# Keys scaled on GpSimd, transfers begun by SP, planned durations reset and weight conversions reordered in a three-layer kernel

## The chip, the cores and the metric

The kernel runs on one core of one Trainium2 chip. The metric is device time in microseconds of the whole program, the median over runs. "Before" and "after" are the kernel without and with the change. Engines are named TensorE (PE in the profile, PEld for its weight loads), VectorE (DVE), ScalarE (ACT), GpSimd (POOL) and SyncE (SP), which only begins transfers here. A row that names "SPq" or "ACTq" speaks of an engine's instruction queue.

## The reference

Three layers in float32, on four sequences of 768 positions and 384 channels. The input of the second and of the third is the output of the one before.

```python
# 1: attention with a decaying state, 8 heads of 48; w, u per head and channel
y[t] = r[t] @ (state + outer(u * k[t], v[t]));  state = w * state + outer(k[t], v[t])
# 2: gate over positions
h = relu(x @ w_in);  u, v = h[..., :512], h[..., 512:]
v = (v - mean(v)) / sqrt(var(v) + 1e-6)
x = (u * (w_spatial @ v + b_spatial)) @ w_out
# 3: gate by a convolution over three positions
h = relu(x @ w_in2);  c = conv3(h, conv_w)
out = (h * sigmoid(c)) @ w_out2
```

`w_in`, `w_out`, `w_in2`, `conv_w` and `w_out2` arrive as 64-bit floats; `w_spatial` as 32-bit ones.

## The kernel before, in words

**Precision.** Every operand of layers 2 and 3 is split into a high part, rounded to the matrix unit's float type by ScalarE (L362), and a low rest, subtracted by GpSimd (L364; both in `hi_lo`). A product is three matmuls (`PARTS`). A piece of 64-bit weights comes by a transfer on SP (L416) into a staging tile `stg`, ScalarE squares its high words (L423), four VectorE instructions make a 32-bit float of it (L427 to L430, in `to_f32`), and `hi_lo` splits it. `split_w` keeps the halves in SBUF (`wi`, `wsp`, `wo`); `split_out` writes them back to memory (L471: `wi2d`, `wo2d`), from where the last stage loads them.

**Attention.** The 768 positions of a sequence are six chunks of 128; there are 24 chunks. Per chunk: two loads on SP (`nat` L498, `ld` L505, three chunks ahead); VectorE multiplies the transposed r and k by a table of decay powers (`scaled`, L572, one instruction for both); GpSimd makes the bonus term in `nat` (L580, L582) and scales the keys in it (L595); VectorE sums it by head (L249) and ScalarE puts it on a diagonal (`aT`, L254). TensorE forms products of queries and keys (`pa`, L216), VectorE copies their upper triangle into `aT` (L610). TensorE then adds the outer product (`pu`, L239), the part from the state (`py`, L222) and the part from the chunk (L231). ScalarE and VectorE split the output into `xT` and `ys` (L647 to L652); the fifth block of rows takes a way through memory, `yd` (L656) and back to `xT` (L661), both issued by ScalarE's queue. In `run`, `att_a(n)` (products) and `att_v(n)` (the rest) alternate in one chain.

**Layer 2.** `s1`: the v half per chunk (L709), then statistics and scaling on VectorE (L722 to L733) and `vn` by `hi_lo`. `s2`: the u half (L751). `s3`: the spatial product (L771), which needs all six `vn` of a sequence, then bias and gate on VectorE and `gat` by `hi_lo`. `s4`: the output (L797) to `x2`, stored in `x2d` by ScalarE's queue (L810).

**Layer 3.** `load2` loads half a sequence (`xl`, L859, on SP); `s5` (L871) with convolution and sigmoid on ScalarE and VectorE (L879 to L891) and `g2` by `hi_lo`; `s6` (L917), ScalarE's copy (L927) and the store of the output, issued by ScalarE's queue (L931). `late_weights` opens the pools of this layer as those of the layers before close: after the attention `w2` (from `wo2d`), after the last `vn` and `u` `w2q` (from `wi2d`), `xl`, `h`, `g`, `o`, and after the last `gat` the PSUM pools and `g2`.

**The order of the work.** All instructions are emitted at build time by `Order`, a planner: each task is a generator that yields needs, slots of buffers and planned durations per engine (`pe`, `pairs`, `dve`, `act`, `gps`, `dma`). The planner always takes the engine that can start earliest and among its ready tasks the one of lowest rank, so that planned durations and ranks fix each engine's instruction order. On the chip each engine then runs its list in that order. `rank(n)` is 0.1 n for the chunks of the first sequence and 1.05 + 0.01 n after; `w_in`'s conversions have 0.55 and 1.1, those of `w_spatial`'s second half, `w_out`, `conv_w`, `w_out2` and `w_in2` (in this order) rank 3 and only after `x` of chunk 3. `keep_warm` (L565) lets TensorE multiply an identity matrix wherever it is idle in the first 62 planned us. The rest of `Net` (`any_decay`) is a second path that these inputs don't take.

## Time and profile before

| | us |
|---|---|
| runs, median of 3 | 609.29 (604.51 to 613.72) |
| the profiled execution | 606.56 |
| its span, first to last instruction | 604.8 |
| TensorE busy | 579.9 (96%) |
| VectorE busy | 399.6 (66%) |
| ScalarE busy | 339.2 (56%) |
| GpSimd busy | 265.5 (44%) |

The span is what the rows divide; 1.8 us of the profiled execution lie around it. Busy shares are averages over stages that differ, and TensorE's holds the filler of `keep_warm`. The granted clock of TensorE was 0.98 of full speed over the span.

### The profile page before, as it was taken

The numbers are of one execution on the slowest core, as the hardware profiler recorded it, in microseconds if no ns is written. First come the engines' busy times: TensorE is split into PE (matmuls) and PEld (weight loads), VectorE is DVE, ScalarE is ACT, GpSimd is POOL, SyncE is SP. The second block draws the span as 40 slices with busy tenths as digits, with TensorE's granted clock in tenths as the row PEclk, the third lists the DMA queues.
The fourth block names the chain that finished last, engine by engine and source line by source line (L and its number), as shares of the span: only waits on it lengthen the run. The fifth ranks groups of instructions, "written<-read, shape, count | busy, mean of one in ns | idle before, by whom it ended". The sixth has DMA issues, their size and how long they took to land.

```text
span 604.8 us, 11115 instructions
## 1 busy us (share of the span) xinstructions
PE 579.9 (96%) x4008; PEld 548.7 (91%) x4008; DVE 399.6 (66%) x864; ACT 339.2 (56%) x853; POOL 265.5 (44%) x292
## 2 busy tenths in 40 slices
PE   6999978899999999997999999999999999999996
PEld 4999968789998999986999899898999999999995
DVE  4689977889788976787865442268465564654640
ACT  4555874567567365663354322188677676766740
POOL 6666785644756354583324232224332342323330
PEclk8999997999999999997999999999999999999998
DMA  8667713667477266573256461522303123030011
GB/s 212 190 204 228 242 39 89 182 189 232 137 217 232 80 207 200 173 242 115 89 162 203 165 233 60 177 80 79 114 18 105 30 90 116 15 105 28 13 44 42
DMA packets 49314, 81.28 MB, mean 134 GB/s; under 512 B 5601, under 2 KB 40930, under 8 KB 48866
## 3 DMA queue, kind: packets, MB, share of 16 engines
q1 hardware_dynamic: 33122, 61.21, 33.3%
q10 hardware_dynamic: 16128, 19.28, 9.3%
q8 instruction: 33, 0.54, 0.4%
q14 instruction: 31, 0.25, 0.1%
HBM read 57.27 MB, written 23.20 MB: 133 GB/s over the span
## 4 chain that ended last, share of the span: by engine, by line
PE 80%; DVE 6%; POOL 5%; issue 4%; ACT 2%; DMA 2%; SPq 0%; ACTq 0%; DVEq 0%; POOLq 0%
PE s L917 17%; PE s L771 15%; PE s L871 15%; PE s L797 7%; PE s L751 6%; PE s L709 6%; PE warm L565 4%; PE pa L216 4%; PE py L231 4%; PE py L222 2%; POOL wsp L364 2%; DVE ld L572 2%; PE pu L239 2%; DMA ld<-in_rkT_dram 1%; POOL vn L364 1%
## 5 line engine op out<-in xcount | busy, mean ns | idle before, releaser
L364 POOL TENSOR_TENSOR g<-g,g 128x384 fp32r<-128x384 f32 x64 | 65.2, 1019 | 127.7 <-ACT g L362 127.7
L771 PE MATMUL s<-wsp,vn 128*128 128x384 f32 x576 | 109.3, 348 | 8.1 <-DVE x L807 4.2
L771 PEld LDWEIGHTS s<-wsp,vn 128*128 128x128 f32 x576 | 104.7, 196 | 10.8 <-DVE x L807 4.6
L871 PE MATMUL s<-xl,wi 128*128 128x386 f32 x576 | 107.9, 340 | 1.2 <-ACT h L879 1.2
L917 PE MATMUL s<-wo,g 128*128 128x384 f32 x576 | 105.8, 337 | 0.0
L871 PEld LDWEIGHTS s<-xl,wi 128*128 128x128 f32 x576 | 102.5, 189 | 1.6 <-ACT h L879 1.6
L917 PEld LDWEIGHTS s<-wo,g 128*128 128x128 f32 x576 | 100.9, 188 | 0.0
L884 DVE SCALAR_TENSOR_TENSOR c<-h,cw,c 128x384 f32<-128x384 f32 x64 | 39.8, 622 | 52.0 <-ACT c L882 52.0
L254 ACT ACTIVATE aT<-ident,dg 128x128 f32<-128x128 f32 x192 | 59.6, 391 | 8.6 <-DVE dg L249 6.1
L364 POOL TENSOR_TENSOR gat<-u,gat 128x384 fp32r<-128x384 f32 x32 | 33.2, 1037 | 55.1 <-ACT gat L362 47.7
L709 PE MATMUL s<-wi,xT 128*128 128x512 f32 x216 | 54.1, 398 | 1.8 <-ACT u L758 1.4
L797 PE MATMUL s<-gat,wo 128*128 128x384 f32 x288 | 54.5, 338 | 1.0 <-POOL gat L364 0.6
L751 PE MATMUL s<-xT,wi 128*128 128x384 f32 x288 | 55.0, 338 | 0.0
L797 PEld LDWEIGHTS s<-gat,wo 128*128 128x128 f32 x288 | 49.9, 188 | 2.3 <-POOL gat L364 0.9
L751 PEld LDWEIGHTS s<-xT,wi 128*128 128x128 f32 x288 | 50.0, 188 | 0.7 <-issue 0.2
L709 PEld LDWEIGHTS s<-wi,xT 128*128 128x128 f32 x216 | 39.8, 189 | 10.7 <-ACT u L758 1.8
L891 DVE TENSOR_TENSOR g<-h,c 128x384 f32<-128x384 f32 x64 | 35.3, 552 | 19.8 <-ACT c L887 18.8
L887 ACT ACTIVATE c<-c 128x384 f32<-128x384 f32 x64 | 29.9, 467 | 31.9 <-DVE c L885 31.9
L572 DVE TENSOR_TENSOR ld<-ld,TT 112x1024 f32<-112x1024 f32 x24 | 41.3, 1723 | 5.4 <-DMA ld<-in_rkT_dram 5.4
L364 POOL TENSOR_TENSOR vn<-v,vn 128x512 fp32r<-128x512 f32 x24 | 31.1, 1303 | 31.1 <-ACT vn L362 31.1
L610 DVE COPY_PREDICATED aT<-mask,pa 128x512 f32<-128x512 uint32 x48 | 34.3, 737 | 15.7 <-PE pa L216 8.8
L362 ACT ACTIVATE gat<-u 128x384 fp32r<-128x384 f32 x32 | 16.7, 523 | 45.9 <-DVE u L780 43.8
(100 smaller groups left out, 900.3 us busy)
## 6 DMA issues: line engine op xcount, KB each, us to landing
nat<-in_rkv_dram SPq DMA_DIRECT2D x24, 576.0 KB, 4.9
ld<-in_rkT_dram SPq DMA_DIRECT2D x24, 448.0 KB, 5.9
xl<-x2d SPq DMA_DIRECT2D x8, 1155.0 KB, 6.1
x2d<-x ACTq DMA_DIRECT2D x24, 384.0 KB, 2.6
stg<-in_w_out_dram SPq DMA_DIRECT2D x24, 192.0 KB, 2.5
out_dram<-o ACTq DMA_DIRECT2D x24, 192.0 KB, 1.9
stg<-in_w_in_dram SPq DMA_DIRECT2D x12, 256.0 KB, 6.0
wo2d<-stg SPq DMA_DIRECT2D x16, 192.0 KB, 2.0
```

The source lines that it names most:

```text
L254: self.nc.scalar.activation(out=a[:, x, h // 2], in_=self.ident, func=ACTF.Copy, scale=d[:, h:h + 1])
L364: nc.gpsimd.tensor_tensor(dst[1], src, dst[0].bitcast(F32), ALU.subtract)
L572: nc.vector.tensor_tensor(ld[n], ld[n], TT, ALU.mult)
L610: nc.vector.copy_predicated(aT[n][:, x], maskb, self.pa[x])
L709: nc.tensor.matmul(out=ps, lhsT=xt[:, k, l], rhs=wi[:, k, r, UF:DFF], start=(k == 0 and (l, r) == PARTS[0]), stop=(k == KD - 1 and (l, r) ...
L751: nc.tensor.matmul(out=ps, lhsT=wi[:, k, l, f * 128:(f + 1) * 128], rhs=xT[b, h][:, k, :, r], start=(k == 0 and (l, r) == PARTS[0]), stop= ...
L771: nc.tensor.matmul(out=ps, lhsT=vn[:, s, l, f * 128:(f + 1) * 128], rhs=wsp[:, s, r, h * HT:(h + 1) * HT], start=(s == 0 and (l, r) == PAR ...
L797: nc.tensor.matmul(out=ps, lhsT=wo[:, k, l, m * 128:(m + 1) * 128], rhs=gat[b, h, k][:, r], start=(k == 0 and (l, r) == PARTS[0]), stop=(k ...
L871: nc.tensor.matmul(out=ps, lhsT=late["wi2"][:, k, l, f * 128:(f + 1) * 128], rhs=xl[j][:, k, r], start=(k == 0 and (l, r) == PARTS[0]), st ...
L884: nc.vector.scalar_tensor_tensor(c, h[:, 0:HT], cw[:, f, 0:1], c, ALU.mult, ALU.add)
L891: nc.vector.tensor_tensor(g, h[:, 1:HT + 1], c, ALU.mult)
L917: nc.tensor.matmul(out=ps, lhsT=g2[j][:, k, l, t * 128:(t + 1) * 128], rhs=late["wo2"][:, k, r], start=(k == 0 and (l, r) == PARTS[0]), st ...
```

## The change

Seven things, all in the functions above:

1. `scaled`: from chunk 1 on VectorE scales the queries alone (512 columns) and a new task `scaled_k` lets GpSimd scale the keys (512 columns). `att_a` needs both, `att_v` the queries.
2. `yd`, `xT`, `x2d` and the output are begun by SP's queue instead of ScalarE's: 24 + 48 + 24 + 24 transfers.
3. Planned durations: `aT`'s diagonal 6 instead of 4 fixed costs, the weights' conversion 5 instead of 4, the chunk's products, state and output parts 1.0 instead of 0.9 us, the outer product 0.45 instead of 0.35, the layer norm 100 and 556 columns more.
4. `att_a` and `att_v` run in two chains.
5. Ranks and order of conversions: `w_in` 0.15 (first six pieces) and 0.35, the first half of `w_spatial` 0.55, then `w_out` and its second half from the start at 1.02; the rest after `w_spatial` is done, with `w_in2` ahead of `conv_w` and `w_out2`.
6. Ranks of tasks: `s1` of the first sequence 0.52, `s2` of the first four tiles 1.05 also behind their first step.
7. `late_weights`: after the attention `w2q`, `xl` and the PSUM pools, after the last `vn` and `u` `h` (6 instead of 8), `g` (5 instead of 6), `o` and `w2`, after the last `gat` only `g2`.

```diff
@@ to_f32
-            yield dve(4 * n, 4)
+            yield dve(4 * n, 5)
...
         def scaled(n):
             yield need(("ldd", n))
-            yield dve(2 * NP * C)
-            nc.vector.tensor_tensor(ld[n], ld[n], TT, ALU.mult)
-            done(("ld", n))
+            if n:
+                spawn(scaled_k(n), rank(n))
+                yield dve(NP * C)
+                nc.vector.tensor_tensor(ld[n][:, 0], ld[n][:, 0], TT[:, 0], ALU.mult)
+                done(("lq", n))
+            else:
+                yield dve(2 * NP * C)
+                nc.vector.tensor_tensor(ld[n], ld[n], TT, ALU.mult)
+                done(("lq", n), ("lk", n))
+
+        def scaled_k(n):
+            yield gps(NP * C)
+            nc.gpsimd.tensor_tensor(ld[n][:, 1], ld[n][:, 1], TT[:, 1], ALU.mult)
+            done(("lk", n))
...
@@ bonus
-                yield act(NP * C, 4)
+                yield act(NP * C, 6)
...
@@ att_a, att_v
-            yield need(("ld", n))
+            yield need(("lq", n), ("lk", n))
...
-            yield od.pairs(0.9)
+            yield od.pairs(1.0)
...
-            yield need(("kn", n), ("z", n - 1))
+            yield need(("lq", n), ("kn", n), ("z", n - 1))
...
-                yield od.pairs(0.35)
+                yield od.pairs(0.45)
...
-            nc.scalar.dma_start(out=yd[n], in_=ys.bitcast(F32).rearrange("p l t -> p (l t)"))
+            nc.sync.dma_start(out=yd[n], in_=ys.bitcast(F32).rearrange("p l t -> p (l t)"))
...
@@ s1
-            yield dve(UF, 3)
+            yield dve(UF + 100, 3)
...
-            yield dve(UF // 2, 4)
+            yield dve(UF + 300, 4)
...
@@ late_weights
             yield need("cw", *[("x", B - 1, c) for c in range(NCH)], *[("z", n) for n in range(n_chunks)][-1:])
+            yield need(*[("wi2d", k, c) for k in range(KD) for c in range(0, DFF, SG)])
+            att.close()
+            wi2 = late["wi2"] = right("w2q", 1, p2).tile([128, KD, 2, DFF], F32R, name="wi2")
...
+            late["xl"] = right("xl", 2, p2)
+            put(xl_f, 2)
+            late["ps"] = p2.enter_context(tc.tile_pool(name="ps6", bufs=2, space=PSUM))
+            late["c"] = p2.enter_context(tc.tile_pool(name="ps_c", bufs=2, space=PSUM))
...
+            ph1a.close()
+            for name, bufs, f in (("h", 6, h_f), ("g", 5, g_f), ("o", 2, o_f)):
+                late[name] = right(name, bufs, p2)
+                put(f, bufs)
             yield need(*[("wo2d", k, c) for k in range(KF) for c in range(0, DM, SG)])
-            att.close()
             wo2 = late["wo2"] = right("w2", 1, p2).tile([128, KF, 2, DM], F32R, name="wo2")
...
@@ run
-            [(s1(b, c), 1) for b in range(B) for c in range(NCH)],
+            [(s1(b, c), 1 if b else 0.52) for b in range(B) for c in range(NCH)],
...
-            spawn(od.chain([(g(n), rank(n)) for n in range(n_chunks) for g in (att_a, att_v)]), 0)
+            for g in (att_a, att_v):
+                spawn(od.chain([(g(n), rank(n)) for n in range(n_chunks)]), 0)
...
-        spawn(in_turn(jobs, lambda i: 0.55 if i < 6 else 1.1), 0.55)
+        spawn(in_turn(jobs, lambda i: 0.15 if i < 6 else 0.35 if i < 12 else 0.55), 0.15)
...
             if xd is None:
                 yield need(("x", 0, 3))
+            yield need(*[("wsp", k, HT) for k in range(NCH)])
             yield from in_turn(tasks, lambda i: 3)
 
-        spawn(later(jobs_w), 3)
+        spawn(in_turn(jobs_o + jobs_w, lambda i: 1.02), 1.02)
         spawn(later(jobs_2), 3)
...
```

## Rows read from the trace of the kernel before

**Rows 1.** The chain that ended last, share of the span by engine and by line.
```profile
PE 80%; DVE 6%; POOL 5%; issue 4%; ACT 2%; DMA 2%; SPq 0%; ACTq 0%; DVEq 0%; POOLq 0%
PE s L917 17%; PE s L771 15%; PE s L871 15%; PE s L797 7%; PE s L751 6%; PE s L709 6%; PE warm L565 4%; PE pa L216 4%; PE py L231 4%; PE py L222 2%; POOL wsp L364 2%; DVE ld L572 2%; PE pu L239 2%; DMA ld<-in_rkT_dram 1%; POOL vn L364 1%
```

**Rows 2.** Stretches: length, busy PE, PEld, DVE, ACT, POOL (instructions), PE clock, DMA, GB/s.
```profile
14.00:58.00 44.00, 44.00 (x494) 40.62 (x495) 35.58 (x68) 25.70 (x81) 26.52 (x30) 0.96 0.70 208
58.00:94.50 36.50, 31.68 (x185) 26.86 (x183) 30.99 (x77) 25.20 (x65) 29.39 (x29) 0.97 0.45 139
94.50:300.00 205.50, 198.80 (x1559) 183.76 (x1560) 167.71 (x386) 114.69 (x334) 111.64 (x123) 0.97 0.57 173
```

**Rows 3.** The same stretches, line L565 (`warm`) alone: length, busy PE, PEld, clock, DMA.
```profile
14.00:58.00 44.00, 26.75 (x196) 24.12 (x196) 0.96 0.70 208
58.00:94.50 36.50, 3.61 (x28) 3.56 (x28) 0.97 0.45 139
```

**Rows 4.** The chain in order of time: start us, us, what.
```profile
93.22 1.29 POOL vn L364
94.55 8.86 PE s L771 x37
...
274.54 5.30 DVE ld L572 x2
280.83 6.13 PE s L771 x18
...
289.12 6.26 PE s L771 x36
```

**Rows 5.** Timeline of PE: start, us, instructions [idle before <-what ended it].
```profile
121.18 1.10 PE L222 MATMUL py<-ld,zbd 112*112 112x128 f32 x8 [1.89 <-DVE xT L651]
...
280.83 6.13 PE L771 MATMUL s<-wsp,vn 128*128 128x384 f32 x18 [4.17 <-DVE x L807]
...
390.20 2.72 PE L797 MATMUL s<-gat,wo 128*128 128x384 f32 x14 [0.64 <-POOL gat L364]
...
413.82 3.47 PE L871 MATMUL s<-xl,wi 128*128 128x386 f32 x18 [1.24 <-ACT h L879]
```

**Rows 6.** Groups by form: count | busy us, mean ns | idle before, releaser.
```profile
L572 DVE TENSOR_TENSOR ld<-ld,TT 112x1024 f32<-112x1024 f32 x24 | 41.3, 1723 | 5.4 <-DMA ld<-in_rkT_dram 5.4
L364 POOL TENSOR_TENSOR vn<-v,vn 128x512 fp32r<-128x512 f32 x24 | 31.1, 1303 | 31.1 <-ACT vn L362 31.1
L428 DVE SCALAR_TENSOR_TENSOR wy<-stg,wy 128x192 uint32<-128x192 uint32 x39 | 14.1, 362 | 1.3
L364 POOL TENSOR_TENSOR wsp<-stg,wsp 128x384 fp32r<-128x384 f32 x12 | 14.2, 1196 | 3.1 <-ACT wsp L362 3.1
L428 DVE SCALAR_TENSOR_TENSOR wy<-stg,wy 128x256 uint32<-128x256 uint32 x12 | 5.1, 429 | 0.4
L364 POOL TENSOR_TENSOR wo<-stg,wo 128x192 fp32r<-128x192 f32 x8 | 4.7, 598 | 1.5 <-ACT wo L362 1.4
```

**Rows 7.** Line L572: count, shortest, median and longest in ns, first and last start.
```profile
L572 DVE TENSOR_TENSOR ld<-ld,TT x24: 1210/1322/4250, 10.4 to 278.6; 112x1024 f32<-112x1024 f32 x24
```

**Rows 8.** Timeline of DVE and POOL from 116 us on.
```profile
116.66 3.70 DVE L572 TENSOR_TENSOR ld<-ld,TT 112x1024 f32<-112x1024 f32 x1
...
117.18 1.00 POOL L364 TENSOR_TENSOR gat<-u,gat 128x384 fp32r<-128x384 f32 x1
...
118.13 1.15 POOL L364 TENSOR_TENSOR wo<-stg,wo 128x192 fp32r<-128x192 f32 x2
```

**Rows 9.** Line L810 on ACT's queue: its waits, shortest, median and longest in ns.
```profile
L810 ACTq EVENT_SEMAPHORE  x10: 17/17/4006, 192.8 to 400.7; - x10
```

**Rows 10.** Waits of SP's queue: us in total, times, longest us.
```profile
SPq L471 <- POOL stg L364: 82.2, 27, 8.9
...
SPq L416 <- POOL wsp L364: 22.4, 8, 12.9
```

**Rows 11.** Transfers: count, KB each, median us from issue to landing.
```profile
yd<-ys ACTq DMA_DIRECT2D x24, 112.0 KB, 3.8
```

More of the change, by code (lines that the diff above doesn't have):

```diff
@@ L622, in att_v @@
             if c:
-                yield od.pairs(0.9)
+                yield od.pairs(1.0)
                 self.from_state(ld[n][:, 0])
@@ L629, in att_v @@
             yield take(ys_f)
-            yield od.pairs(0.9)
+            yield od.pairs(1.0)
             del ld[n]
@@ L660, in att_v @@
                 r0 = x * OB
-                nc.scalar.dma_start(
+                nc.sync.dma_start(
                     out=xt[r0 + D:r0 + OB].bitcast(F32).rearrange("p k l t -> p k (l t)"),
@@ L809, in s4 @@
             yield dma(1024 * HT)
-            nc.scalar.dma_start(out=x2d[b, :, m, :, h * HT:(h + 1) * HT], in_=x2.bitcast(F32))
+            nc.sync.dma_start(out=x2d[b, :, m, :, h * HT:(h + 1) * HT], in_=x2.bitcast(F32))
             done(("x2d", b, h, m))
@@ L820, in late_weights @@
             yield need("cw", *[("x", B - 1, c) for c in range(NCH)], *[("z", n) for n in range(n_chunks)][-1:])
+            yield need(*[("wi2d", k, c) for k in range(KD) for c in range(0, DFF, SG)])
+            att.close()
+            wi2 = late["wi2"] = right("w2q", 1, p2).tile([128, KD, 2, DFF], F32R, name="wi2")
+            for k in range(KD):
+                yield dma(1024 * DFF)
+                nc.sync.dma_start(out=wi2[:, k].bitcast(F32), in_=wi2d[:, k])
+            done("wi2")
+            late["xl"] = right("xl", 2, p2)
+            put(xl_f, 2)
+            late["ps"] = p2.enter_context(tc.tile_pool(name="ps6", bufs=2, space=PSUM))
+            late["c"] = p2.enter_context(tc.tile_pool(name="ps_c", bufs=2, space=PSUM))
+            put(ps6_f, 2)
+            put(c_f, 3)
+            yield need(*[("vn", B - 1, c) for c in range(NCH)], *[("u", B - 1, h, f) for h in range(2) for f in range(KU)])
+            ph1a.close()
+            for name, bufs, f in (("h", 6, h_f), ("g", 5, g_f), ("o", 2, o_f)):
+                late[name] = right(name, bufs, p2)
+                put(f, bufs)
             yield need(*[("wo2d", k, c) for k in range(KF) for c in range(0, DM, SG)])
-            att.close()
             wo2 = late["wo2"] = right("w2", 1, p2).tile([128, KF, 2, DM], F32R, name="wo2")
@@ L827, in late_weights @@
             done("wo2")
-            yield need(*[("vn", B - 1, c) for c in range(NCH)], *[("u", B - 1, h, f) for h in range(2) for f in range(KU)])
-            yield need(*[("wi2d", k, c) for k in range(KD) for c in range(0, DFF, SG)])
-            ph1a.close()
-            wi2 = late["wi2"] = right("w2q", 1, p2).tile([128, KD, 2, DFF], F32R, name="wi2")
-            for k in range(KD):
-                yield dma(1024 * DFF)
-                nc.sync.dma_start(out=wi2[:, k].bitcast(F32), in_=wi2d[:, k])
-            done("wi2")
-            for name, bufs, f in (("xl", 2, xl_f), ("h", 8, h_f), ("g", 6, g_f), ("o", 2, o_f)):
-                late[name] = right(name, bufs, p2)
-                put(f, bufs)
             yield need(*[("gat", B - 1, h, f) for h in range(2) for f in range(KU)])
             ph1b.close()
-            late["ps"] = p2.enter_context(tc.tile_pool(name="ps6", bufs=2, space=PSUM))
-            late["c"] = p2.enter_context(tc.tile_pool(name="ps_c", bufs=2, space=PSUM))
             late["g2"] = p2.enter_context(tc.tile_pool(name="g2", bufs=2))
-            put(ps6_f, 2)
-            put(c_f, 3)
             put(g2_f, 2)
@@ L930, in s6 @@
                 t0 = h * HT + t * 128
-                nc.scalar.dma_start(out=self.out[b, t0:t0 + 128], in_=o)
+                nc.sync.dma_start(out=self.out[b, t0:t0 + 128], in_=o)
                 put(o_f)
@@ L949, in run @@
         jobs += [split_w(wsp, self.w_spT, k, 0, HT, by_gat, "wsp") for k in range(NCH)]
-        jobs_2 = [split_w(wo, self.w_out, k, c * SG, SG, by_sg, "wo") for k in range(KU) for c in range(DM // SG)]
+        jobs_o = [split_w(wo, self.w_out, k, c * SG, SG, by_sg, "wo") for k in range(KU) for c in range(DM // SG)]
         jobs_w = [split_w(wsp, self.w_spT, k, HT, HT, by_sg, "wsp") for k in range(NCH)]
+        jobs_2 = [split_out(wi2d, self.w_in2, k, c, min(SG, DFF - c), by_sg, "wi2d")
+                  for c in range(0, DFF, SG) for k in range(KD)]
         jobs_2 += [conv_weights(by_sg)]
@@ L954, in run @@
                    for k in range(KF) for c in range(0, DM, SG)]
-        jobs_2 += [split_out(wi2d, self.w_in2, k, c, min(SG, DFF - c), by_sg, "wi2d")
-                   for c in range(0, DFF, SG) for k in range(KD)]
         def load_b():
@@ L1010, in run @@
             spawn(od.chain(c), r)
-        spawn(od.chain([(s2(*x), 1.9) for x in bhf[:KU]]), 1.05)
+        spawn(od.chain([(s2(*x), 1.05) for x in bhf[:KU]]), 1.05)
         spawn(od.chain(m3), 2.5)
```

## The prediction

> **What bounds the kernel now.** I read four views in this order: the chain that ended last, the busy times by stage, the chain in order of time, and the groups of the engines that the chain leaves TensorE for.
>
> The chain by engine is 80% TensorE, 6% VectorE, 5% GpSimd [rows 1]. So the order of TensorE's work decides most of the time, and a faster engine beside it pays only where TensorE waits or does filler. The same chain by line has 4% in `warm` L565, 2% each in GpSimd's `wsp` L364 and VectorE's `ld` L572: about 25, 12 and 12 us of 604.8. `warm` computes nothing that is needed.
>
> By stage [rows 2]: from 14 to 58 us TensorE is busy throughout, from 58 to 94.5 us for 31.7 of 36.5 us. But L565 alone has 26.8 and 3.6 us of that [rows 3]. Of these 80.5 us, 30.4 are filler and 80.5 - 44.0 - 31.7 = 4.8 are idle, so that 45.3 us are needed work and 35 us could go at the very most. The other engines say what paces this stage: VectorE is busy 35.6 + 31.0 = 66.6 of 80.5 us, GpSimd 26.5 + 29.4 = 55.9, and the DMA engines run at 0.70 of their time in the first part. The stage ends when the spatial product of batch 0 runs freely, at 94.55 us, right behind GpSimd's last `vn` [rows 4].
>
> After 94.5 us TensorE is nearly always busy. The idle stretches that I find are 1.9 us at 121, behind the residual copy of a chunk's output; 4.2 us at 281, followed by 18 matmuls in 6.13 us where 36 of the same line take 6.26 [rows 4, 5], which is 6.13 - 3.13 = 3.0 us more; 0.6 us at 390, behind the last gates; and 1.2 us at 414, where the last stage starts. That is 9.1 us at boundaries between batches and 1.9 us at the change to the last stage. What is left is matmuls back to back and a tail of some 5 us; the change touches neither.
>
> **The change part by part.**
>
> *Keys scaled by GpSimd.* Now one VectorE instruction of 1024 columns scales both halves: 24 times, 1.72 us each, 41.3 us [rows 6]. For 23 chunks it becomes a VectorE instruction of 512 columns and a GpSimd one. The shortest of the 24 took 1.21 us [rows 7], so the half costs between 0.61 us (half of that) and 1.21 us (if all of it were fixed); I take 0.65, nearest to the half. GpSimd's price for 512 columns is 1.30 us (`vn` L364) [rows 6]. The trace shows why the mean is 1.72 and not 1.21: at 116.66 us one took 3.70 us while GpSimd ran one multiplication after another until 119.28 us, and it ended 1.08 us behind the last of them [rows 8]. GpSimd's pair of `wo` took 1.15 us there, no more than two of 0.60, so VectorE is what stood.
>
> The Trainium skill says it as a rule (SBUF — State Buffer, "SBUF: two separate sides"): VectorE with two inputs in SBUF and GpSimd share one port pair as an exclusive lock, and whichever starts first keeps it for its whole instruction. Here the trace agrees, with 3.70 us against 1.21. The rule speaks against this edit, since both halves are released by the same transfer and would take the lock in turn: 0.65 + 1.30 = 1.95 us for the pair, more than the 1.72 now.
>
> From the rows, then: VectorE saves between 1.72 - 0.65 = 1.07 us and -0.23 us (1.72 - 1.95, when it stands behind the keys) per chunk; I take 0.5, since the mean blocked time is already 0.51 us with GpSimd 69% busy and its share rises. Nine chunks are scaled in the first stage (the six of batch 0 and three loaded ahead), one of them as before: VectorE -4 us, GpSimd +8 x 1.3 = +10.4 us.
>
> *Weights converted in another order.* In the first stage the conversions of `w_in` get a rank ahead of chunks 2 to 5, where before they came behind all of batch 0. Each piece is four VectorE instructions of 0.43 us [rows 6], 1.7 us, 12 pieces: 20.5 us. They are not less, but they fill VectorE's gaps in the first part of the stage, so that the v projections (L709) can stand where `warm` stands. The second halves of `w_spT` leave the stage (five pieces on GpSimd, 1.20 us each: -6.0) and pieces of `w_out` may enter it: up to six more, 4 x 0.36 us on VectorE (+8.6) and 0.60 on GpSimd (+3.6) [rows 6], but at a rank that only takes gaps. Sum for the stage: VectorE 66.6 - 4 = 62.6 us, 71.2 with all of `w_out`; GpSimd 55.9 + 10.4 - 6.0 + 3.6 = 63.9. If the fuller of the two is 95% busy, against VectorE's 83% now, the stage takes 63.9/0.95 = 67 us (75 us with all of `w_out`) instead of 80.5: 13 or 5.5 us less. Bounds: 0 (utilisation stays at 83%) and 16 us (no filler and no lock). I take -11.
>
> *Two chains for the attention.* A chunk's products no longer stand behind the preceding chunk's state and output. TensorE is never idle there, so this pays only by letting needed work replace filler; it is in the 11 us. It costs nothing on TensorE: the same matmuls. The masks on VectorE are what comes late next.
>
> *Boundaries.* At 281 us the chain goes through two `ld` L572 of 5.30 us together just ahead of the wait [rows 4]; halves would be about 2.5. With longer planned durations for the layer norm and `aT`, the plan also puts fewer matmuls ahead of data that isn't there. Of 9.1 us I take 5, bounds 0 and 9.
>
> *Late weights.* `w_in2`, its tiles and the two PSUM pools come ahead of `w_out2`, so the last stage can begin while the last gates still run. TensorE's own work is unchanged; only the 1.9 us of idling can go: -1.5, bounds 0 and 2. The smaller pools (`h` 6, `g` 5) cost nothing as long as at most three `c` tiles are in flight, which the plan sets; the cover would be gone if GpSimd fell five tiles behind.
>
> *Transfers on SP.* 120 issues leave ScalarE. Its longest wait for one was 4.0 us, on `x2d` [rows 9]; ScalarE isn't on the chain there, so nothing is booked for it. On SP they stand behind whatever waits there: `wi2d` and `wo2d` stores waited 82 us in 27 waits (8.9 at most) for GpSimd, stage loads 22 us (12.9 at most) [rows 10]. Queued behind such a wait would be `yd`, `xT` and `x2d`, and behind `xT`, which needs `yd` landed (3.8 us [rows 11]), the loads of the next chunk. Bounds 0 (chunks are loaded three ahead) and +9 us for one wait at a batch's end; I take +2, near 0 since most of these waits are SP being early.
>
> **Sum.** The profiled execution took 606.56 us (604.8 span and 1.8 around it). -11 - 5 - 1.5 + 2 = -15.5 gives 591.1 us. The median of the runs shown is 609.29, 2.7 us above the profiled one; in its ratio 591.1 becomes 593.7. I predict 594 us. Own range: best terms -16 - 9 - 2 + 0 = -27, or 582; worst 0 + 0 + 0 + 2 (the 9 us are a rival, below), or 611.
>
> **Rivals.**
>
> *The port takes it back.* The keys on GpSimd and VectorE's instructions block each other, so that VectorE saves nothing. For: 3.70 us beside 1.21 [rows 7, 8]. Against: the median is 1.32 us, so most don't meet. VectorE's sum for the stage is then 66.6 us, or 75.2 with all of `w_out`; at 95% the stage takes 70 or 79 us, 10 or 1.5 less, and I take 4, nearer to the fuller case since VectorE's blocked time counts as busy. The boundary at 281 us stays but for 1 us: -4 - 1 - 1.5 + 2 = -4.5, 602.1 or 605 us in the median's terms. The rule of the Trainium skill cited above (SBUF — State Buffer, "SBUF: two separate sides") leads to this case.
>
> *Slower: SP's queue holds the last transfers of a batch.* Place: the `yd` and `xT` of a batch's last chunk behind a stage load or store that waits for a GpSimd conversion. For: waits of 8.9 and 12.9 us on SP, and GpSimd is fuller afterwards. Against: now no wait of TensorE for `xT` shows at all. It decides as soon as the last v projection is what TensorE reaches first; at 8 us a batch it costs 4 x 8 = 32 us against the 15.5 gained: +16.5, 623.1 or 626 us.
>
> *It doesn't do what it says.* The plan's durations are no cause by themselves, and a different order puts as many waits elsewhere as it removes: +1, 607.6 or 610 us.
>
> **How the numbers follow.** Forecast 0.58, port 0.24, SP queue 0.13, no effect 0.05. The bound of 2% (about what a measurement of this kernel can tell from no change) lies at 597.1 and 621.5 us. The forecast's case lies mostly below 597, with some of it above (0.05), and a little of the port case lies below (0.05): faster 0.58. Within 2%: 0.19 + 0.05 + 0.05 and a fifth of the SP case, 0.31. Slower 0.11. The range takes in the forecast's bounds and the port case: 581 to 610.
>
> **What would show it.** Right: `warm` falls from 30 us to under 18; L771 runs freely by about 84 us; the wait at 281 us is under 2 us; VectorE's `ld` has a mean near 1.2 us. Wrong: GpSimd over 90% busy up to 90 us with the filler kept (port); TensorE's or ScalarE's waits named `xT<-yd` (SP queue). The forecast falls if the stage's end does not move by at least 5 us.

## The result, and the profile after

| | before | after |
|---|---|---|
| runs, median | 607.59 us (20 runs) | 611.99 us (20 runs) |
| ratio after / before | | 1.0081, 95% interval 1.0060 to 1.0101 |
| the profiled execution, its span | 606.56, 604.8 us | 615.76, 614.0 us |
| TensorE's last matmul ends | 599.06 us | 601.00 us |
| from there to the end of the span | 5.7 us | 13.0 us |

By the ratio the change makes the kernel 4.9 us slower (the two medians differ by 4.4): 612 us, where 594 were forecast and the range ended at 610. The last line of the table holds more than that: 7.3 us behind the last matmul, a place that the prediction had left out of its sum. The trace of after is of the longest of its 20 executions. Experiment 1 below is the same program but for the queue of the output stores, which all come behind 400 us; experiment 4 also begins the other transfers by ScalarE's queue. In both every engine computes the same instructions in the same order as in after, so their traces show by how much the figures of one execution can be off.

The page of after, busy time of each engine and the chain that ended last by engine:

```profile
PE 581.4 (95%) x3992; PEld 548.0 (89%) x3992; DVE 406.6 (66%) x864; ACT 340.4 (55%) x853; POOL 291.8 (48%) x315
PE 73%; DVE 6%; issue 3%; POOL 3%; DMA 2%; ACT 1%; SPq 0%; DVEq 0%; POOLq 0%; ACTq 0%
```

VectorE was to be relieved; it is busy 7 us longer than before (5 us longer in experiment 1, 1 us less in experiment 4), and GpSimd 26 us longer. In the chain GpSimd falls from 5% to 3% [rows 1], and VectorE keeps its 6%.

The stretches of after, columns as in [rows 2]:

```profile
14.00:58.00 44.00, 44.00 (x442) 40.48 (x440) 36.89 (x78) 28.47 (x86) 33.81 (x38) 0.94 0.70 217
58.00:94.50 36.50, 32.17 (x232) 27.10 (x228) 32.71 (x79) 20.57 (x56) 28.48 (x28) 0.96 0.43 127
94.50:300.00 205.50, 198.53 (x1570) 180.86 (x1570) 164.61 (x357) 113.02 (x326) 127.06 (x131) 0.97 0.52 161
```

and the filler `warm` L565 alone in the first two, as in [rows 3]:

```profile
14.00:58.00 44.00, 23.32 (x172) 21.90 (x172) 0.94 0.70 217
58.00:94.50 36.50, 4.87 (x36) 4.39 (x36) 0.96 0.43 127
```

Two things are to be seen. In the first stage VectorE is busy 36.9 + 32.7 = 69.6 of 80.5 us (66.6 before), GpSimd 33.8 + 28.5 = 62.3 (55.9 before), and the filler falls only from 30.4 to 28.2 us. From 94.5 to 300 us TensorE idles 205.5 - 198.5 = 7.0 us (4.4 in experiment 1, 3.2 in experiment 4), and before it was 6.7.

The groups of after that hold the moved work (count | busy us, mean ns | idle before), with VectorE's halves L574, the layer norm's scaling L744 (L733 before) and GpSimd's keys L583:

```profile
L574 DVE TENSOR_TENSOR ld<-ld,TT 112x512 f32<-112x512 f32 x23 | 41.6, 1811 | 1.7 <-DMA ld<-in_rkT_dram 1.7
L744 DVE TENSOR_SCALAR v<-v,mv,rs 128x512 f32<-128x512 f32 x24 | 22.5, 936 | 1.7
...
L583 POOL TENSOR_TENSOR ld<-ld,TT 112x512 f32<-112x512 f32 x23 | 31.0, 1346 | 1.4 <-DMA ld<-in_rkT_dram 1.3
```

The layer norm's scaling in before, which no row above shows:

```profile
L733 DVE TENSOR_SCALAR v<-v,mv,rs 128x512 f32<-128x512 f32 x24 | 17.2, 716 | 1.8
```

and shortest, median and longest of the two lines in after, in ns:

```profile
L574 DVE TENSOR_TENSOR ld<-ld,TT x23: 653/1200/4482, 14.4 to 290.2; 112x512 f32<-112x512 f32 x23
...
L744 DVE TENSOR_SCALAR v<-v,mv,rs x24: 545/547/2472, 66.8 to 355.6; 128x512 f32<-128x512 f32 x24
```

In this execution half the columns cost VectorE as much as the whole did: 41.6 us for 23 halves beside 41.3 us for 24 wholes [rows 6]. The price of the half alone was forecast well (0.65 us; the shortest is 0.653). The rest is standing, time in which an instruction has begun and gets no further: 41.6 - 23 x 0.653 = 26.6 us, where before it was 41.3 - 24 x 1.210 = 12.3. The neighbour that was not counted, L744, pays too: 5.3 us more for the same 24 instructions.

How much is standing differs between executions. The halves in experiment 1 and in experiment 4:

```profile
L574 DVE TENSOR_TENSOR ld<-ld,TT 112x512 f32<-112x512 f32 x23 | 36.1, 1575 | 1.9 <-DMA ld<-in_rkT_dram 1.9
...
L574 DVE TENSOR_TENSOR ld<-ld,TT 112x512 f32<-112x512 f32 x23 | 33.0, 1440 | 1.9 <-DMA ld<-in_rkT_dram 1.9
```

That is 21.1 and 18.0 us of standing. With the one whole of chunk 0 (1.5 us) counted, the scaling of r and k costs VectorE 1.8 us more than before in after's trace, and 3.7 and 6.9 us less in these two, where 23 x 0.5 = 11.5 us less were forecast. The layer norm's scaling takes 25.4 and 21.8 us there.

What it stands behind is to be seen in after's timeline of VectorE, GpSimd and TensorE (start us, us, ...):

```profile
118.88 3.94 DVE L574 TENSOR_TENSOR ld<-ld,TT 112x512 f32<-112x512 f32 x1
122.75 0.28 DVE L661 TENSOR_TENSOR ys<-py,ys 112x128 fp32r<-112x128 f32 x1
...
118.09 1.02 POOL L593 TENSOR_TENSOR nat<-nat,uB 128x384 f32<-128x384 f32 x1
119.05 1.31 POOL L583 TENSOR_TENSOR ld<-ld,TT 112x512 f32<-112x512 f32 x1
120.30 1.02 POOL L606 TENSOR_TENSOR nat<-nat,Tnat 128x384 f32<-128x384 f32 x1
121.27 2.41 POOL L364 TENSOR_TENSOR gat<-u,gat 128x384 fp32r<-128x384 f32 x2
...
123.63 1.10 PE L222 MATMUL py<-ld,zbd 112*112 112x128 f32 x8 [2.50 <-DVE xT L662]
...
250.03 1.16 PE L216 MATMUL pa<-ld 48*128 48x128 f32 x16 [2.63 <-POOL gat L364]
...
283.59 1.10 PE L222 MATMUL py<-ld,zbd 112*112 112x128 f32 x8 [1.27 <-DVE xT L662]
```

The two halves of a chunk are released by one transfer, so they can meet. VectorE's 0.65 us of work begins at 118.88 us, while GpSimd is in an instruction begun at 118.09, and ends 3.94 us later, after the keys, the next multiplication and most of a pair behind it. Behind it the split of the output is late, and TensorE waits 2.50 us; in before that place cost 1.89 [rows 5]. The wait at 281 us has shrunk from 4.17 to 1.27, and a new one of 2.63 stands at 250.

The Trainium skill (SBUF — State Buffer, "SBUF: two separate sides") says that whichever of the two engines starts first holds the shared ports for its whole instruction. These rows agree that the two block each other; but more than the one instruction that had started first goes by before VectorE's turn comes.

The end of the chain in order of time, after:

```profile
578.73 22.27 PE s L931 x126
...
601.07 0.50 ACT o L941
...
601.59 0.33 SPq L945
...
602.01 1.50 DMA wt<-in_w_dram
...
603.61 0.56 DVE wt L1052
...
604.19 0.54 DVE lim L1053
604.73 0.46 DVE lim L1054
605.19 0.07 DVE lim L1055
...
605.28 0.15 DVE flag L1056
```

and what follows on that flag in after (shortest, median and longest in ns, then first and last start):

```profile
L1058 PEldq TENSOR_LOAD <-flag x1: 494/494/494, 605.5 to 605.5; - x1
...
L1059 PEldq COMPARE_BRANCH  x1: 4342/4342/4342, 606.1 to 606.1; - x1
...
L1059 SPq EVENT_SEMAPHORE  x8: 17/17/17, 609.3 to 612.3; - x8
```

Behind `net.run()` the program loads the decay `w` on SP (L1051), tests its range in five VectorE instructions, and each engine loads the flag and branches on it: that decides whether the second path runs. In SP's list this load stands behind the last of the output stores. In before SP had none of these stores and began it at 579.7 us, beside the last product, and TensorE's branch ran from 596.4 to 599.9. After, the load waits for ScalarE's last copy, and everything behind it lies bare: 1.5 us of load, 1.8 of VectorE, 0.5 of flag, and then two things side by side. TensorE's branch takes 4.3 us and ends at 610.4; SP has branched at 606.0, and the last of its eight semaphore events comes at 612.3, later than TensorE's branch. What those events wait for, no row shows. In before the last of them came at 603.5, 1.3 us ahead of the end.

### The profile page after: what moved, and what is told of

Its sections match the earlier page's. It is cut to its first block, busy times and chain, and to the rows that moved or that the text cites. A ratio compares the mean times of both kernels' runs of the same rounds, so it can differ in the third digit from the quotient of the medians.

```text
span 614.0 us, 11147 instructions
## 1 busy us (share of the span) xinstructions
PE 581.4 (95%) x3992; PEld 548.0 (89%) x3992; DVE 406.6 (66%) x864; ACT 340.4 (55%) x853; POOL 291.8 (48%) x315
## 3 DMA queue, kind: packets, MB, share of 16 engines
q1 hardware_dynamic: 49250, 80.48, 41.6%
## 4 chain that ended last, share of the span: by engine, by line
PE 73%; DVE 6%; issue 3%; POOL 3%; DMA 2%; ACT 1%; SPq 0%; DVEq 0%; POOLq 0%; ACTq 0%
PE s L885 17%; PE s L931 17%; PE s L782 14%; PE s L808 7%; PE s L762 6%; PE s L720 6%; PE pa L216 2%; PE py L231 2%; PE py L222 2%; DVE ld L574 1%; DMA nat<-in_rkv_dram 1%; POOL vn L364 1%; DVE v L744 1%; PE pu L239 1%; DMA yd<-ys 1%
## 5 line engine op out<-in xcount | busy, mean ns | idle before, releaser
L782 PE MATMUL s<-wsp,vn 128*128 128x384 f32 x576 | 109.3, 344 | 5.9 <-POOL vn L364 3.2
L782 PEld LDWEIGHTS s<-wsp,vn 128*128 128x128 f32 x576 | 101.8, 192 | 10.3 <-POOL vn L364 5.0
L898 DVE SCALAR_TENSOR_TENSOR c<-h,cw,c 128x384 f32<-128x384 f32 x64 | 39.7, 621 | 55.9 <-ACT c L896 55.9
L364 POOL TENSOR_TENSOR gat<-u,gat 128x384 fp32r<-128x384 f32 x32 | 33.8, 1064 | 54.1 <-ACT gat L362 51.7
L720 PE MATMUL s<-wi,xT 128*128 128x512 f32 x216 | 56.6, 414 | 0.0
L720 PEld LDWEIGHTS s<-wi,xT 128*128 128x128 f32 x216 | 41.5, 198 | 9.9 <-ACT zbd L245 0.4
L901 ACT ACTIVATE c<-c 128x384 f32<-128x384 f32 x64 | 29.8, 466 | 30.6 <-DVE c L899 30.5
L574 DVE TENSOR_TENSOR ld<-ld,TT 112x512 f32<-112x512 f32 x23 | 41.6, 1811 | 1.7 <-DMA ld<-in_rkT_dram 1.7
L893 ACT ACTIVATE h<-s 128x386 f32<-128x386 f32 x64 | 31.4, 491 | 18.3 <-PE s L885 17.4
L899 DVE SCALAR_TENSOR_TENSOR c<-h,cw,c 128x384 f32<-128x384 f32 x64 | 39.9, 623 | 2.3
```

What stands on the lines that cost most here:

```text
L364: nc.gpsimd.tensor_tensor(dst[1], src, dst[0].bitcast(F32), ALU.subtract)
L574: nc.vector.tensor_tensor(ld[n][:, 0], ld[n][:, 0], TT[:, 0], ALU.mult)
L720: nc.tensor.matmul(out=ps, lhsT=xt[:, k, l], rhs=wi[:, k, r, UF:DFF], start=(k == 0 and (l, r) == PARTS[0]), stop=(k == KD - 1 and (l, r) ...
L782: nc.tensor.matmul(out=ps, lhsT=vn[:, s, l, f * 128:(f + 1) * 128], rhs=wsp[:, s, r, h * HT:(h + 1) * HT], start=(s == 0 and (l, r) == PAR ...
L898: nc.vector.scalar_tensor_tensor(c, h[:, 0:HT], cw[:, f, 0:1], c, ALU.mult, ALU.add)
L899: nc.vector.scalar_tensor_tensor(c, h[:, 2:HT + 2], cw[:, f, 2:3], c, ALU.mult, ALU.add)
```

## The experiments

All ratios are against the kernel before, and medians are of 6 to 12 runs. Where a line of code is named without more, it is that of after.

**1. The output stores alone go back.** After, with one line undone:

```diff
-                nc.sync.dma_start(out=self.out[b, t0:t0 + 128], in_=o)
+                nc.scalar.dma_start(out=self.out[b, t0:t0 + 128], in_=o)
```

> The changed kernel with only the 24 output stores back on ScalarE's queue. Theory (the end): the test of the decay values stands at the end of SP's list, so with the output stores on SP its load waits for the last store; this costs 13.0 - 5.7 = 7.3 us behind TensorE's last matmul. Expected: the load of the 1.5 KB starts near 580 us again, 5 to 6 us lie between TensorE's last matmul and the end, span near 606.7, ratio to the kernel before 0.99 to 1.00. Rival (the middle: the stage up to 94 us and the boundaries lost what was gained): the end is an accident of this trace, span stays at 612 to 614 and the ratio at 1.008.

603.3 us, ratio 0.9938 [0.9915, 0.9961]: 8.7 us less than after's 611.99, from slower than before to faster. Its last matmul ends at 595.42 and its span at 600.4, so 5.0 us lie behind instead of 13.0. These 8.0 us are the gain but for 0.7.

**2. The stores stay on SP, the test moves.** After, with the load and the five VectorE instructions ahead of `net.run()`:

```diff
-            net.run()
             with tc.tile_pool(name="fw", bufs=1) as fw:
...
                     flag, lim[:, 1:2], W2_MAX, lim[:, 2:3], ALU.is_gt, ALU.max)
+            net.run()
```

> The changed kernel with the test of the decay values (one load, five VectorE instructions) moved ahead of everything else; the output stores stay on SP. Theory (the end): it is the test's place behind the stores that costs, not the stores on SP: 5 to 6.5 us between TensorE's last matmul and the end instead of 13.0, ratio 0.99 to 1.00, less up to 2 us that the test costs at the start. Rival (output stores on SP are slow to land or to be waited for): the end stays above 10 us and the ratio at 1.005 or more.

605.8 us, ratio 0.9970 [0.9943, 0.9997]: 6.2 us of the 8.7 come back. The tail is 7.7 us, where 5 to 6.5 were expected. What is left shows in the branch lines of this kernel:

```profile
L1059 PEldq COMPARE_BRANCH  x1: 3742/3742/3742, 597.3 to 597.3; - x1
L1059 ACTq COMPARE_BRANCH  x1: 50/50/50, 600.6 to 600.6; - x1
L1059 SPq COMPARE_BRANCH  x1: 53/53/53, 601.0 to 601.0; - x1
...
L1059 SPq EVENT_SEMAPHORE  x8: 17/17/17, 603.9 to 606.3; - x8
```

TensorE's branch is covered again, but SP's own comes at 601.0, behind the last store, and SP's eight semaphore events behind it run until 606.3 (in before SP branched at 584.6 and the last of these came at 603.5). So it seems that a store on SP delays the end even without the test, by SP's late branch. That was read from these rows of one execution and not tried, and the intervals of experiments 1 and 2 overlap.

**3. The stores alone, in before.**

```diff
-                nc.scalar.dma_start(out=self.out[b, t0:t0 + 128], in_=o)
+                nc.sync.dma_start(out=self.out[b, t0:t0 + 128], in_=o)
```

> The kernel before with only the 24 output stores moved to SP. Theory (the end): all of the loss and none of the rest, +7.3 us: ratio 1.010 to 1.014, 13 us behind TensorE's last matmul. Rival (the middle): ratio 1.000 within 0.003.

612.21 us, ratio 1.0105 [1.0065, 1.0145]: 6.4 us lost by this line alone. The end of its chain is that of after:

```profile
577.30 21.87 PE s L917 x126
...
600.18 1.58 DMA wt<-in_w_dram
...
603.54 0.15 DVE flag L1040
```

With the three together the end is shown, but for the 2.5 us that experiment 2 leaves: undone, gone round, and done alone.

**4. The other transfers go back too.** Experiment 1, with `yd`, `xT` and `x2d` on ScalarE's queue again.

```diff
-            nc.sync.dma_start(out=yd[n], ...
+            nc.scalar.dma_start(out=yd[n], ...
```

> The changed kernel with all four kinds of transfers back on ScalarE's queue (output, x2d, yd, xT). Against e1_out_on_act this tells what x2d, yd and xT cost or bring on SP. Theory (SP's waits delay the loads of chunks): 1 to 4 us faster than e1_out_on_act, ratio 0.987 to 0.992. Rival (ScalarE is freed of waits of up to 4 us, worth something): slower by 1 to 3 us, ratio 0.995 to 0.999.

604.7 us, ratio 0.9947 [0.9911, 0.9983], beside 0.9938 in experiment 1 and between the two ranges expected. Ninety-six transfers in the middle of the program neither cost nor bring anything that can be measured; the 24 at its end cost 8.7 us.

**5. The keys alone, in before.** Part 1 of the change and nothing else.

```diff
+                spawn(scaled_k(n), rank(n))
+                yield dve(NP * C)
+                nc.vector.tensor_tensor(ld[n][:, 0], ld[n][:, 0], TT[:, 0], ALU.mult)
```

> The kernel before with only the keys of 23 chunks scaled by GpSimd. Theory (the port takes it back): the VectorE half has a mean of 1.6 to 1.9 us although it is half as long, VectorE's busy time falls by less than 5 us, and the time is the same or up to 4 us worse: ratio 0.998 to 1.007. Rival (the forecast's step: 0.5 us saved per chunk): mean near 1.2 us, ratio 0.99 to 0.997.

612.51 us, ratio 1.0082 [1.0054, 1.0111]. VectorE's groups in this kernel:

```profile
L574 DVE TENSOR_TENSOR ld<-ld,TT 112x512 f32<-112x512 f32 x23 | 33.7, 1465 | 0.0
L744 DVE TENSOR_SCALAR v<-v,mv,rs 128x512 f32<-128x512 f32 x24 | 22.4, 934 | 1.8
```

The halves save 41.3 - 33.7 - 1.5 (chunk 0) = 6.1 us, the layer norm gives 5.2 of it back, and TensorE idles 10.9 us between 94.5 and 300 us instead of 6.7. So this edit, which was to relieve the engine that the forecast's largest term rests on, costs time by itself, a little more than the theory had (1.007 at most), though the mean of 1.47 us lies between the theory's and the rival's. The edit also changes the plan's order; how much of the loss is blocking and how much is order, this run does not tell.

**6. The keys back on VectorE, in after.** Experiment 1 and:

```diff
-            if n:
-                spawn(scaled_k(n), rank(n))
...
+            yield dve(2 * NP * C)
+            nc.vector.tensor_tensor(ld[n], ld[n], TT, ALU.mult)
+            done(("lq", n), ("lk", n))
```

> The changed kernel with the output stores on ScalarE (as in e1_out_on_act) and the keys scaled by VectorE in the one instruction of before. Theory (the port takes the keys' gain back): GpSimd's share of the scaling bought nothing, so this is 2 to 6 us faster than e1_out_on_act: ratio to the kernel before 0.984 to 0.991. Rival (VectorE was relieved, if by little): slower than e1_out_on_act, ratio 0.995 to 1.00.

599.28 us, ratio 0.9854 [0.9781, 0.9926]. The middle of this kernel:

```profile
94.50:300.00 205.50, 203.60 (x1623) 186.59 (x1620) 169.77 (x372) 115.28 (x335) 117.08 (x122) 1.00 0.54 165
```

TensorE idles 1.9 us there, at a granted clock of 1.00, where after has 7.0 at 0.97. But the filler is 29.5 us and the first stage is no shorter, so it isn't the stage that pays. The interval overlaps that of experiment 1: that the keys' way back gains is likely, not shown.

**7. One chain for the attention.** Experiment 1 with part 4 undone.

```diff
-            for g in (att_a, att_v):
-                spawn(od.chain([(g(n), rank(n)) for n in range(n_chunks)]), 0)
+            spawn(od.chain([(g(n), rank(n)) for n in range(n_chunks) for g in (att_a, att_v)]), 0)
```

> The changed kernel with the output stores on ScalarE and products and the rest of a chunk in one chain again. Theory (two chains pay only where needed work replaces filler): within 2 us of e1_out_on_act, ratio 0.990 to 0.997. Rival (two chains are what gained): 5 us slower or more, ratio 1.002 or more.

605.43 us, ratio 0.9975 [0.9936, 1.0015]. This lies between the two ranges expected. The two chains may be worth some 2 us; the intervals overlap.

**8. The old durations.** Experiment 1 with part 3 undone; then the same with the keys on VectorE.

```diff
-            yield od.pairs(1.0)
+            yield od.pairs(0.9)
...
-            yield dve(UF + 300, 4)
+            yield dve(UF // 2, 4)
```

> The changed kernel with the output stores on ScalarE and all planned durations as before. Theory (durations fitted to the trace avoid waits): 2 to 5 us slower than e1_out_on_act, ratio 0.997 to 1.002. Rival (the durations only deal the waits anew): within 1.5 us either way, ratio 0.991 to 0.996.

> The changed kernel with the output stores on ScalarE, the keys scaled by VectorE and the planned durations as before: the parts that cost are undone, the order of conversions, the two chains, the late weights and three kinds of transfers on SP stay. If the gains of e5_keys_vector (0.9854) and e8_old_durations (0.9879) against e1_out_on_act (0.9938) add: 0.979 to 0.981. Rival (each only deals the waits anew): 0.985 to 0.992.

600.7 us, ratio 0.9879 [0.9819, 0.9940], and with the keys on VectorE 605.3, 0.9957 [0.9927, 0.9987]. Each step alone looks like a gain over experiment 1 (the intervals overlap), and the two together give none: VectorE's scaling then takes 49.8 us for 24 wholes (2073 ns each), beside 41.2 in experiment 6. The durations taken from the trace did not make a better plan.

**9. The old ranks and order of conversions.** Experiment 1 with parts 5 and 6 undone (`w_in2` still ahead of `w_out2`); then the same with the keys on VectorE.

```diff
-        spawn(in_turn(jobs, lambda i: 0.15 if i < 6 else 0.35 if i < 12 else 0.55), 0.15)
+        spawn(in_turn(jobs, lambda i: 0.55 if i < 6 else 1.1), 0.55)
...
-        spawn(in_turn(jobs_o + jobs_w, lambda i: 1.02), 1.02)
-        spawn(later(jobs_2), 3)
+        spawn(later(jobs_w), 3)
+        spawn(later(jobs_o + jobs_2), 3)
```

> The changed kernel with the output stores on ScalarE, and the order of part 5 and 6 of the change undone: w_in's conversions at 0.55 and 1.1, the second half of w_spatial and w_out late, s1 at 1 and s2 at 1.9; w_in2 stays ahead of w_out2. Theory (the new order brings nothing by the end of the first stage, which came only 1 us earlier): within 3 us of e1_out_on_act, ratio 0.989 to 1.000. Rival (the new order is what gains outside the end): 6 us slower or more, ratio above 1.003.

> The changed kernel with the output stores on ScalarE, the keys scaled by VectorE, and the order of parts 5 and 6 undone (e5_keys_vector and e10_old_ranks together). If the two gains over e1_out_on_act (0.8% and 0.5%) add: 0.979 to 0.982. Rival (VectorE's scaling in one piece gains only with the new order): 0.987 to 0.993.

601.04 us, ratio 0.9889 [0.9847, 0.9930], and 602.54, 0.9908 [0.9874, 0.9943]. In the first of them the spatial product runs freely, without further stops for a `vn`, only from 98.17 us, 6.2 us later than in experiment 1 (91.97; 93.45 in after, whose program is the same up to there), and the kernel is no slower. So the end of the first stage, on which the forecast was built, is not what the time follows: what isn't done there is done later.

**10. The old order of the late weights.** Experiment 1 with part 7 undone, and `conv_w` and `w_out2` ahead of `w_in2`.

```diff
             yield need(*[("wo2d", k, c) for k in range(KF) for c in range(0, DM, SG)])
             att.close()
...
-            for name, bufs, f in (("h", 6, h_f), ("g", 5, g_f), ("o", 2, o_f)):
+            for name, bufs, f in (("xl", 2, xl_f), ("h", 8, h_f), ("g", 6, g_f), ("o", 2, o_f)):
```

> The changed kernel with the output stores on ScalarE, and late_weights as before (w_out2 first, pools of 8 and 6, the last stage only after the last gates) with conv_w and w_out2 converted ahead of w_in2. Theory (the last stage started without waits in the changed kernel: 2 us): 1.5 to 4 us slower than e1_out_on_act, ratio 0.996 to 1.001. Rival (late weights bring nothing): ratio 0.991 to 0.995.

603.31 us, ratio 0.9928 [0.9901, 0.9955]. The waits are back (0.63 us at 389.87, 0.96 at 413.19, against 0.64 and 1.24 in [rows 5]), and the time is that of experiment 1.

**11. Half the filler.** Experiment 6 with one multiplication of the identity matrix per planned step instead of two. This leaves out half of `warm`'s matmuls, which compute nothing that is needed.

```diff
-                for j in range(2):
+                for j in range(1):
```

> The changed kernel with the output stores on ScalarE and the keys scaled by VectorE (as in e5_keys_vector), and keep_warm writing one matmul where it wrote two, so that half the filler is left out and the plan stays the same. Theory (the first stage is paced by the conversions, the loads and VectorE's and GpSimd's lists, and filler only fills): the spatial product of batch 0 still starts within 2 us of e5_keys_vector, TensorE idles instead, time within 3 us of it. Rival (TensorE's own list, filler included, paces the first stage): 14 us of filler go and the stage ends 5 to 12 us earlier, ratio 0.966 to 0.978.

594.41 us, ratio 0.9789 [0.9747, 0.9831], the fastest kernel of the study, though its interval still overlaps that of experiment 6. Its first two stretches, from the longest of its seven executions (599.63 us at a mean granted clock of 0.975; the others took 593.97 to 595.86 at 0.981 to 0.992):

```profile
14.00:58.00 44.00, 37.71 (x368) 32.80 (x368) 38.28 (x79) 28.45 (x87) 29.78 (x32) 0.93 0.71 217
58.00:94.50 36.50, 34.03 (x208) 29.68 (x207) 30.97 (x82) 20.93 (x57) 26.37 (x27) 0.83 0.44 129
```

TensorE idles 6.3 us in the first and is granted 0.83 in the second, against 0.98 in experiment 6; still the spatial product begins its free run 2 us earlier, at 92.68 instead of 94.67 us, and the filler takes 20.1 us of these stretches instead of 29.5. But after and experiment 1 differ by 1.5 us at this point with the same program up to there, so that the filler stood in the way is not shown by these 2 us, nor is what the lower clock cost. Shown is that half of it can go without loss.

**12. `w_out` behind the first stage.** In experiment 1 the chain of the first stage went through a load of `w_out` (6.15 us from 70.30) that ScalarE awaited ahead of a `v` tile. The theory was that without `w_out` the stage would end early. Experiment 1 with `w_out` held back until the last `vn` of the first sequence, which also lets the second half of `w_spatial` come into the stage in its place; then the same with the keys on VectorE and half the filler.

```diff
-        spawn(in_turn(jobs_o + jobs_w, lambda i: 1.02), 1.02)
+        def behind():
+            yield need(("vn", 0, NCH - 1))
+            yield from in_turn(jobs_o, lambda i: 1.02)
+
+        spawn(in_turn(jobs_w, lambda i: 1.02), 1.02)
+        spawn(behind(), 1.02)
```

> The changed kernel with the output stores on ScalarE (as e1_out_on_act) and w_out's eight pieces begun only behind the last vn of batch 0, with the second half of w_spatial ahead of them. Theory (w_out in the first stage is what holds its end: in e1_out_on_act ScalarE stood 6 us at the square of a w_out piece that had not landed, in front of the eviction of v): the free run of the spatial product of batch 0 starts at 84 to 88 us instead of 92, ratio 0.984 to 0.991. Rival (the stage is held by VectorE's layer norms and the port): 90 us or later, ratio 0.991 to 0.998.

> As e13_w_out_behind, with the keys scaled by VectorE and half the filler left out (as e9_half_filler). If the gain of e13 adds to e9 (0.979): 0.970 to 0.976. If it only deals the waits anew: 0.977 to 0.985.

625.23 us, ratio 1.0280 [1.0242, 1.0317], and 630.14, 1.0357 [1.0317, 1.0396]. The theory falls: the spatial product begins at 91.59 us, no earlier than in experiment 1, though the last `vn` ends 3.5 us earlier (88.4 instead of 91.9): TensorE has products of the attention ahead of it. And `w_out` then comes late, as TensorE's timeline of the first of the two shows:

```profile
145.41 2.08 PE L216 MATMUL pa<-ld 48*128 48x128 f32 x16 [5.80 <-DVE ld L574]
...
163.16 6.63 PE L808 MATMUL s<-gat,wo 128*128 128x384 f32 x27 [7.74 <-ACT wo L362]
```

TensorE idles 23.9 us from 94.5 to 300 us. GpSimd begins the last piece of `w_out` at 166.4 us here, at 118.7 in before, at 100.0 in after, and at 129.3 in the first kernel of experiment 9, which loses nothing. So what costs is `w_out` as late as here; that its early place in the change is worth anything, no run shows.

## Why the prediction was wrong

Put together, the idle time of TensorE from 94.5 to 300 us (205.5 less its busy time, one profiled execution each) goes with the ratio at the two ends of this list of kernels whose end is that of before. Beside it stands TensorE's granted clock in that stretch:

| kernel | idle us, 94.5 to 300 | clock | ratio |
|---|---|---|---|
| 11, half the filler | 1.4 | 0.99 | 0.9789 |
| 9, old ranks, keys on VectorE | 1.3 | 0.98 | 0.9908 |
| 6, keys on VectorE | 1.9 | 1.00 | 0.9854 |
| 8, old durations | 1.9 | 0.98 | 0.9879 |
| 4, all transfers back | 3.2 | 0.98 | 0.9947 |
| 1, stores back | 4.4 | 0.99 | 0.9938 |
| 9, old ranks | 4.8 | 0.98 | 0.9889 |
| 10, old late weights | 5.3 | 0.98 | 0.9928 |
| 8, old durations, keys on VectorE | 6.1 | 0.99 | 0.9957 |
| before | 6.7 | 0.97 | 1 |
| 7, one chain | 8.0 | 0.99 | 0.9975 |
| 5, before with keys on GpSimd | 10.9 | 0.98 | 1.0082 |
| 12, `w_out` behind | 23.9 | 0.93 | 1.0280 |
| 12, with keys on VectorE, half the filler | 30.5 | 0.88 | 1.0357 |

This is an observation across kernels: no run changed that idle time and nothing else. After and experiment 1, the same program up to 300 us, idle 7.0 and 4.4 us; before and experiment 3, likewise, 6.7 and 7.6. So rows less than some 3 us apart can't be put in order by one trace each.

The change without its end saves 0.0062 x 607.6 = 3.8 us (interval 2.4 to 5.2), the end costs 8.7, and 4.9 is what was measured. The forecast had -15.5.

**The end.** The step that turned the sign is one sentence: "What is left is matmuls back to back and a tail of some 5 us; the change touches neither." The change moved 24 stores onto the queue that begins the test behind the kernel, and the tail became 13.0 us. The part on SP named `yd`, `xT`, `x2d` and the chunk loads as what would be queued behind a wait, and none of what comes last in SP's list. Of its +2 us for the middle nothing can be measured (experiment 4); it lacked +8.7 at the end. The rival "SP's queue holds the last transfers of a batch" had the right queue in the wrong place: no wait of TensorE for `xT<-yd` shows in after.

**The first stage, -11 us.** About -1, and at best -2.6: the free run of the spatial product begins at 93.45 us instead of 94.55, at 91.97 in experiment 1. The sums of busy time were right (VectorE 62.6 to 71.2 forecast, 69.6 found; GpSimd 63.9 and 62.3), VectorE's partly by luck: the scaling saved it 2.1 us in the stage (12.7 to 10.6), not 4. Two steps failed. The 0.5 us that VectorE was to save per chunk: the mean went from 1.72 to 1.81 us (1.58 and 1.44 in experiments 1 and 4), and the layer norm became 0.22 us a chunk dearer on top (0.34 and 0.19). And the 95% that the fuller engine was to be busy: VectorE came to 69.6 of 80.5 us, 86%, after 83% before. The chain says why. Before, from 64 to 95 us, by line:

```profile
by line: POOL wsp L364 29.9%; POOL vn L364 19.7%; issue 19.3%; POOL wi L364 8.4%; DMA stg<-in_w_spT_dram 7.3%; POOL nat L580 3.3%; POOL nat L582 3.2%; PE s L771 2.2%; ACT v L716 1.9%; ACT wsp L362 1.7%; POOL zc L681 1.5%; POOL nat L595 1.4%
```

and after, the same stretch in order of time:

```profile
74.28 4.28 DVE ld L574 x2
...
84.19 1.67 DVE v L744
...
89.75 1.64 DVE v L744
91.41 0.64 ACT vn L362
...
92.12 1.29 POOL vn L364
```

Before, GpSimd with `w_spatial`, `w_in` and `vn` was last; the forecast took for the engine that paces the one with the most busy time. The change takes that work away from the stretch, and VectorE's layer norms come to the same place, on a chain that holds two halves of 4.28 us together (1.3 unblocked) and two scalings of 1.67 and 1.64 us (0.55 unblocked). That is 3.0 + 2.2 = 5.2 us of standing behind GpSimd on the path itself. The two scalings are on it in experiment 1 as well (2.23 and 1.64 us); in place of the halves it has the load of `w_out` there (6.15 us), so the halves' part is not on the path of every execution. Besides, experiment 9 shows that an earlier or later end of this stage need not move the total.

**Boundaries, -5 us.** The wait at 281 us went below 2 us as forecast, but little of that by the reason given: the two `ld` ahead of it took 1.49 and 3.00 us, together 4.5 instead of the 2.5 forecast and the 5.30 before [rows 4]. The sum is nothing: 6.7 us of idling became 7.0, with a longer wait at 123 and a new one at 250. The 3.0 us that the 18 matmuls behind the wait took too long have moved likewise. TensorE was granted 0.50 (1.2 GHz) from 280.3 to 287.0 us in before; in after it has 1.00 there, and 0.50 from 125.4 to 128.7 and from 251.7 to 255.0, behind the waits of 2.50 and 2.63 us. The rival "it doesn't do what it says" had put it so, "a different order puts as many waits elsewhere as it removes", and was given 0.05.

**Late weights, -1.5 us.** The two waits went, as forecast, and no time with them (experiment 10).

**The signs named beforehand.** `warm` under 18 us: 28.2, wrong. L771 (now L782) free by 84 us: 93.45, wrong. The wait at 281 under 2 us: right. `ld` near 1.2 us: 1.81, wrong. GpSimd over 90% busy with the filler kept, the sign of blocking: the filler was kept with GpSimd at 77% (62.3 of 80.5), so blocking doesn't need a full GpSimd. The rival "the port takes it back" had the mechanism right, and its 605 us are close to the change without its end (603.3), by luck in part: it counted -4 for the stage, -1 for the boundaries, -1.5 for the late weights and +2 for SP, and of these only the stage's is found in part.

**Open.** Which part of the change brings the 3.8 us that it saves without its end is not shown: each part undone alone left the time as it was or shorter, but for the two chains, whose 2 us lie within the intervals. Whether keys on GpSimd help or harm depends on the order around them: +0.8% from before to experiment 5 and from 6 to 1, nothing between the two of 9, -0.8% between the two of 8. Only the first of these is clear of its interval. How often the two engines' instructions meet may decide it; no run settles that, nor which order is best.

## What to carry to other kernels

When transfers change queues, read the new queue's list to its last entry, and the program's end most of all: something small that ran early and free may stand there, and everything behind it becomes bare. Before work is moved from VectorE to GpSimd, compare the shortest instruction of each line with its mean on VectorE, for the neighbours too; what is above the shortest was already standing here, and two halves that one event releases can meet. And look for the idle time of the bounding engine in the whole program, not for one stage's end: the planner dealt the waits anew at each edit here, and gains of single edits did not add. And read a few us off a trace only beside a second execution: here one line's total was 36.1 us in one and 41.6 us in another, with no change to the program up to that line's last instruction.

## What the runs showed of the hardware that was not expected

A TENSOR_SCALAR of VectorE (L744, one tensor, two scalars per partition, both from SBUF) stands behind GpSimd like the two-input multiplication: 0.545 us alone, 2.472 at the longest (begun at 188.37 us, beside GpSimd instructions of 1.29 and 1.28 us begun at 188.03 and 189.28). The branch at the end took TensorE 4.34 us in after, where it had been idle since 601.0 us and was granted 0.50 (1.2 GHz) from 604 us on, 4.30 us in experiment 3, whose end is the same, and 3.50 to 3.74 us in before and in experiments 1 and 2, where it lay beside the last matmuls; the other engines' branches took 0.05 to 0.07. The clock in after's tail, third column from the end:

```profile
604.00:608.00 4.00, 0.00 (x0) 0.00 (x0) 1.36 (x5) 0.00 (x0) 0.00 (x0) 0.50 0.06 12
608.00:613.00 5.00, 0.00 (x0) 0.00 (x0) 0.00 (x0) 0.00 (x0) 0.00 (x0) 0.50 0.04 11
```

And executions of one kernel differ with the granted clock: of experiment 6 one took 593.84 us at a mean clock of 0.995 and one 602.01 at 0.984, so single profiled spans that differ by a few us say little.
